# A delta-rule attention with a hardswish feed-forward on one core: one relu of each block a unit later, and the last results in joined stores

## The chip, the cores and the metric

The kernel runs on one core of one Trainium2 chip. The metric is device time in microseconds, from launch to end. A profile of one execution is used beside it; its span runs from the first to the last instruction of the program.

## The reference

```python
for t in range(S):                                   # attention: B=4, H=8, S=768, D=48
    kt, vt, bt = k_n[:, :, t], v[:, :, t], beta[:, :, t, None]     # k_n: keys by their norm
    y[:, :, t] = einsum('bhd,bhde->bhe', q[:, :, t], state)
    v_old = einsum('bhde,bhd->bhe', state, kt)
    state = state + bt[..., None] * einsum('bhd,bhe->bhde', kt, vt - v_old)
x = y.transpose(0, 2, 1, 3).reshape(B * S, H * D)    # 3072 tokens of 384
h = x @ w_in                                         # 384 x 2048
g = h * clip(h + 3, 0, 6) / 6
out = g @ w_out                                      # 2048 x 384, out is 3072 x 384, float32
```

## The kernel before

**Steps and blocks.** The sequence is cut into N = 24 steps `t` of C = 32 tokens. A step holds the 32 tokens of all four batches, 128 rows, which fill the 128 partitions: batch by batch, 32 partitions each. Two steps (CB = 2) make a block of 256 rows, `blk` from 0 to 11, and the feed-forward part runs by blocks. `chain(t)` is the sequential part of a step on TensorE, with copies on ScalarE (ACT) and sums on VectorE (DVE). Its last part, the generator `output()`, makes `y`, transposes it on TensorE into the PSUM tile `yt` (L873), and ScalarE copies that to the step's half of the block's `xT` (L877). In `y` the batches of a pair stand exchanged: batch b is on the partitions of b ^ 1 (`of_heads(py, lambda b: b ^ 1, ...)`, L857).

**The first product.** From block UF = 5 on, `up_by_eleven(blk)` makes x @ w_in. It takes 2 x 2 parts of the operands with seven products in place of eight, and the third 128 rows of w_in with four more: eleven in all. `token_sums(blk)` (L1056, DVE) makes the sums of tokens that this needs out of `xT`, just before. The work is split into NPR = 8 pairs `j` of columns. Of a pair, `begin(j)` issues the first four products into a PSUM bank `ph` (L1066), a copy to `g` on ScalarE (L1080) and two sums on GpSimd (L1030); `end(j)` issues the rest and two sums on DVE (L1093, L1097). Then the pair has two more pieces, which `go(j)` calls one after the other:

- `first`: ScalarE copies the last quarter out of the bank (L1100), which sets the bank free, and makes relu(g / 6 + 1/2) into a scratch tile (L1104).
- `rest`: DVE makes min(relu, 1) times g (L1107, called `go(j)` a second time).

The scratch tile `ro` has the name `o` and one buffer, and so has the tile `o` of the block's results. The first relu of a block therefore waits for the stores of the previous block, and each relu for the L1107 of the pair before it.

**The second product.** From block 2 on `down_by_seven(blk)` makes g @ w_out by seven products (L1218), with copies out of PSUM on ScalarE (L1225) and sums of the parts (L1228) on GpSimd, or on DVE in the last block. Its results stand in `o`, 128 rows by two steps by 384. `to_dram(t, o)` (L1143) stores one step's: a DMA for each batch, 32 rows of 384 floats, all on SP's queue, in the last two steps the odd batches on ScalarE's queue.

**Order.** The order of instructions is written by the program. For the first five steps it is the string `ORDER`; from step LS = 5 on, each step has NU = 15 units: in each, `plan[u]` issues pieces of attention (the chain, and `prep` of a later step: transposes of keys and queries on TensorE into `pt`, L524, and their copies `KQ` on ScalarE, L532), and then `take(units)` issues one unit of the feed-forward part. The yields in `up_by_eleven` part its units. Each engine runs its instructions in the order of issue, and waits for semaphores where an operand is not ready. PSUM banks of the tag `pm` (four) are shared by `ph`, `pt`, `po`, `pz`, `py` and `yt`.

Of the kernel before, what the change touches and what calls it, by code (L numbers as in the profile page):

```python
# [14 lines left out]
ACTF = mybir.ActivationFunctionType  # L15
# [29 lines left out]
def kernel(  # L45
# [21 lines left out]
    nc = tc.nc  # L67
    B, H, S, D = q.shape
    DM, FF = moe_w_in.shape
    C, DP = 32, 64  # L70
    P = B * C
    assert P == 128 and S % C == 0 and D <= DP and H % 2 == 0
    N = S // C
# [6 lines left out]
    CB = 2  # L80
# [14 lines left out]
    def rows(b):  # L95
        return slice(C * b, C * b + C)
# [40 lines left out]
    def needs(*what):  # L137
        assert past.issuperset(what), (what, set(what) - past)
# [5 lines left out]
    def ring(tag, n, key):  # L144

        held = rings.setdefault(tag, [])
        i = len(held)
        if i < n:
            held.append(key)
        else:  # L150
            i = min(range(n), key=lambda i: reads.get(held[i], len(reads)))
            needs(("read", held[i]))
            held[i] = key
        slot[tag] = f"{tag}{i}"

    def read(*keys):
        for key in keys:
            past.add(("read", key))
            reads.setdefault(key, len(reads))
# [53 lines left out]
    for j, value in enumerate((1.0, -1.0)):  # L213
        m = mask2[:, j, :]
        for b in range(B):
            nc.gpsimd.memset(mask2[rows(b), j, :], value)
            nc.gpsimd.affine_select(
                out=mask2[rows(b), j, :], in_=mask2[rows(b), j, :], pattern=[[1, C]],
# [96 lines left out]
    for i, n in enumerate((0, 1, 2, 3, 4, 5, 0, 1, 3, 4, 5, 0, 1, 5, 0, 1)):  # L315
        s, f = weights[i][0].shape[1:]
# [458 lines left out]
    xTs, outs, zs = {}, {}, {}  # L775
# [8 lines left out]
    def by_pair(t):  # L784
        return t.rearrange("p (a e w) -> p e a w", e=2, w=D)

    def chain(t, whole=True):
# [29 lines left out]
        def plus(out, ph, sign, into):  # L817
            for e in range(2):
                nc.vector.scalar_tensor_tensor(
                    out=by_pair(out)[:, e], in0=ph[:, e], scalar=sign, in1=by_pair(into)[:, e],  # L820
                    op0=ALU.mult, op1=ALU.add,
                )

        def of_heads(ps, place, m, z, at=lambda h: h):
            for h in range(H):
                for b in range(B):
                    nc.tensor.matmul(  # L827
                        ps[rows(place(b)), D * h : D * h + D],
                        lhsT=m(h)[rows(b)], rhs=z[rows(b), D * at(h) : D * at(h) + D],
                        start=True, stop=True, skip_group_check=True,  # L830
                        tile_position=(C * b, C * place(b)),
                    )
# [4 lines left out]
        def output(Z=None):  # L837

            if t > 0:
                needs(("turned", t - 1))  # L840
            y = work.tile([P, DM], FP32, name="y", bufs=1)
            if t > 0:
                nc.scalar.activation(
                    out=by_pair(y[:]), in_=even, func=ACTF.Copy, scale=parity[:, 1, 1:2]
                )
                past.add(("even", t))
                if ("R", t) in past:
                    read(("ks", t, 0))
                yield 1
                plus(y[:], odd, parity[:, 0, 1:2], y[:])  # L850
                read(*(("ks", t, i) for i in range(2)))
                yield
            needs(("Z", t))
            Z = zs.pop(t)
            ring("pm", NPM, ("py", t))
            py = psM.tile([P, 512], FP32, name="py", tag=slot["pm"])
            of_heads(py, lambda b: b ^ 1, lambda h: LB[:, he(h), :], Z)  # L857
            past.add(("BZ", t))
            yield
            if t == 0:  # L860
                nc.scalar.activation(out=y[:], in_=py[:, 0:DM], func=ACTF.Copy)
            else:
                nc.vector.tensor_tensor(out=y[:], in0=y[:], in1=py[:, 0:DM], op=ALU.add)
            read(("py", t))
            yield
            blk, cc = divmod(t, CB)
            if cc == 0:
                needs(*([("up", blk - 2)] if blk >= 2 else []))
                xTs[blk] = work.tile([128, NKT, TB], FP32, name="xT")
            ring("pm", NPM, ("yt", t))  # L870
            pt = psM.tile([128, NKT, P], FP32, name="yt", tag=slot["pm"])
            for s in range(NKT):
                nc.tensor.transpose(pt[:, s, :], y[:, s * 128 : (s + 1) * 128], ident[:])  # L873
            past.add(("turned", t))
            yield 1
            read(("yt", t))
            nc.scalar.activation(  # L877
                out=xTs[blk][:, :, cc * P : (cc + 1) * P], in_=pt[:], func=ACTF.Copy
            )
            past.add(("seam", t))  # L880
            yield

# [11 lines left out]
        else:  # L894
# [5 lines left out]
            for e in range(2):  # L900
                nc.vector.scalar_tensor_tensor(
                    out=Rp[:, e].rearrange("p (a w) -> p a w", w=D), in0=even[:, e],
# [4 lines left out]
            if whole:  # L907
                yield
            nc.vector.scalar_tensor_tensor(
                out=Rp, in0=odd.rearrange("p e a w -> p e (a w)"), scalar=parity[:, 1, 0:1],  # L910
# [43 lines left out]
        for i, x in enumerate(su):  # L954
            sv = state[:, 2 * i : 2 * i + 2].rearrange("p b a w -> p b (a w)")
            nc.vector.tensor_tensor(
                out=sv, in0=sv, in1=x[:, :, 0 : NP * D], op=ALU.subtract
# [101 lines left out]
    def up_by_eleven(blk):  # L1059
        needs(("sums", blk))  # L1060
        B11, T3x, B21, B22, _, _ = x_tiles(blk)
        B3 = xTs[blk][:, 2].rearrange("p (i c) -> p i c", c=P)
        phs, ready = {}, {}

        def mm(ph, n, w, x, start=False, stop=False):
            nc.tensor.matmul(  # L1066
                ph[:, n], lhsT=w, rhs=x, start=start, stop=stop, skip_group_check=True
            )

        def begin(j):  # L1070
            key = ("ph", blk, "by", j)
            ring("pm", NPM, key)
            ph = phs[j] = psM.tile([128, 4, P], FP32, name="ph", tag=slot["pm"])
            mm(ph, 0, W11[:, j], B11, start=True)
            mm(ph, 1, S1[:, j], T1x)
            mm(ph, 2, W21[:, j], T3x)
            mm(ph, 3, S2[:, j], T2x)
            gs[blk, j] = g_all[:, 2 * j : 2 * j + 2]
            gt = gs[blk, j].rearrange("p i (t c) -> p (i t) c", c=P)
            nc.scalar.activation(out=gt, in_=ph[:], func=ACTF.Copy)  # L1080
            plus_minus(gt[:, 3:1:-1], gt[:, 0:2], gt[:, 3:1:-1], ALU.add)
            plus_minus(gt[:, 0], gt[:, 0], gt[:, 2], ALU.add)

        def end(j):
            ph = phs.pop(j)
            mm(ph, 0, W12[:, j], B21)
            mm(ph, 1, S4[:, j], B22)
            mm(ph, 2, W22[:, j], T4x)
            mm(ph, slice(0, 2), W13[:, j], B3)
            mm(ph, slice(2, 4), W23[:, j], B3, stop=True)  # L1090
            g = gs[blk, j].rearrange("p i c -> p (i c)")
            gt = gs[blk, j].rearrange("p i (t c) -> p (i t) c", c=P)
            nc.vector.tensor_tensor(  # L1093
                out=gt[:, 1:3], in0=ph[:, 1:3],
                in1=gt[:, 3].unsqueeze(1).to_broadcast([128, 2, P]), op=ALU.add,
            )
            nc.vector.tensor_tensor(out=gt[:, 3], in0=ph[:, 3], in1=gt[:, 0], op=ALU.add)  # L1097

            def first():
                nc.scalar.activation(out=gt[:, 0], in_=ph[:, 0], func=ACTF.Copy)  # L1100
                read(("ph", blk, "by", j))
                ro = mlp.tile([128, CB, DM], FP32, name="o", bufs=1)
                r = ro[:].rearrange("p c m -> p (c m)")[:, 0 : 2 * TB]
                nc.scalar.activation(out=r, in_=g, func=ACTF.Relu, bias=half, scale=1.0 / 6.0)  # L1104

                def rest():
                    nc.vector.scalar_tensor_tensor(  # L1107
                        out=g, in0=r, scalar=1.0, in1=g, op0=ALU.min, op1=ALU.mult
                    )

                ready[j] = rest

            ready[j] = first
            if j == NPR - 1:
                past.add(("up", blk))

        def go(j):
            if j in ready:
                ready.pop(j)()

        begin(0)
        yield
        begin(1)
        yield
        for j in range(NPR):
            end(j)
            go(j - 1)
            if j + 2 < NPR:
                yield
                begin(j + 2)  # L1130
                go(j)
                yield
            else:
                go(j)
                if j == NPR - 1:
                    go(j)
                yield

    def to_dram(t, o):
        for b in range(B):  # L1140
            r0 = b * S + t * C
            eng = nc.scalar if t >= N - CB and b % 2 else nc.sync
            eng.dma_start(out=out[r0 : r0 + C, :], in_=o[rows(b ^ 1)])  # L1143

    def down(blk, c, f0):

# [294 lines left out]
    with tc.manual_schedule():  # L1441
# [15 lines left out]
        for t in range(LS, N):  # L1457
            g, i = group(t)
# [29 lines left out]
            ready = (2, 0) if behind or i == 2 and t - LS == LA - LE else (1, 6)  # L1488
# [62 lines left out]
```

## Time and profile before

| | |
|---|---|
| median of 3 runs | 667.11 us (666.32 to 667.86) |
| profiled execution | 665.93 us, its span 664.1 us |
| mean granted TensorE clock | 0.974 |
| TensorE (PE) | 636.2 us busy, 96% of the span |
| DVE, ACT, POOL | 487.1, 272.1 and 203.5 us busy |
| DMA queues | q1 (SP) 31.29 MB, q10 (ScalarE) 0.30 MB |
| stores to `out` | 92 from SP, 4 from ScalarE, 48.0 KB each |

A line of a timeline has the start in us from the span's start, the duration, the engine, the source line, the operation, output <- inputs and shapes, the count of merged instructions, and in brackets the idle time of the engine just before and what ended it. A line of the waits has who waited, for whom, the us in total, the times and the longest. SPq and ACTq are the instruction queues of SyncE and ScalarE, which issue DMAs; they are not counted as busy. PEld is the load of weights into TensorE.

### The profile page before, as it was taken

Reading aid. Unit: us, or ns where it says so; the run is one execution under the profiler, and the core shown is the slowest. Engines: PE = TensorE matmul, PEld = TensorE weight load, DVE = VectorE, ACT = ScalarE, POOL = GpSimd, SP = SyncE. Lnnn points to the kernel's source line nnn. Section 1 sums busy time; section 2 is a strip of 40 time slices with the busy share of each in tenths; the row PEclk is TensorE's granted clock in tenths of the full one; section 3 lists DMA queues with packets and bytes.
Section 4 is the critical chain, followed back from the end, with each engine's and each line's share of the span. In section 5 each row is a group of like instructions: output and inputs, shape, how many; then the busy total and the mean of one; then the engine's idle time right before and its main releaser. Section 6 shows DMA issues by size and latency. Waiting matters only on the chain.

```text
span 664.1 us, 26330 instructions
## 1 busy us (share of the span) xinstructions
PE 636.2 (96%) x11544; PEld 568.1 (86%) x11544; DVE 487.1 (73%) x1146; ACT 272.1 (41%) x532; POOL 203.5 (31%) x320
## 2 busy tenths in 40 slices
PE   2769999999999999999999999999999999999997
PEld 1658987776789989989989999999999999999997
DVE  4899867898555697657979748989658998456353
ACT  5897679331233143142144244244244144153350
POOL 6531112003511320562254354064052241331430
PEclk9659999999999999999999999999999999999999
DMA  7897246212140030041030030020020020000000
GB/s 175 206 236 197 76 98 161 49 28 41 23 83 8 10 66 3 2 85 27 2 74 3 2 74 3 3 61 2 3 50 2 2 50 1 23 19 2 25 1 25
DMA packets 88499, 33.27 MB, mean 50 GB/s; under 512 B 80160, under 2 KB 83232, under 8 KB 88384
## 3 DMA queue, kind: packets, MB, share of 16 engines
q1 hardware_dynamic: 88128, 31.29, 20.9%
q8 instruction: 91, 1.49, 0.9%
q10 hardware_dynamic: 256, 0.30, 0.2%
q14 instruction: 24, 0.20, 0.1%
HBM read 26.84 MB, written 4.72 MB: 48 GB/s over the span
## 4 chain that ended last, share of the span: by engine, by line
PE 90%; DVE 3%; DMA 2%; SPq 2%; ACT 1%; issue 1%; POOL 0%; ACTq 0%; DVEq 0%; POOLq 0%
PE po L1218 28%; PE ph L1066 20%; PE ph L994 16%; PE po L1154 6%; PE ks L806 3%; PE pt L524 3%; PE su L938 3%; PE pz L827 3%; PE py L827 3%; PE sc L547 3%; PE yt L873 1%; DMA spare<-in_moe_w_in_dram 1%; PE pi L684 1%; DMA w_out<-in_moe_w_in_dram 1%; SPq L168 1%
## 5 line engine op out<-in xcount | busy, mean ns | idle before, releaser
L1066 PE MATMUL ph<-xT,w_in 128*128 128x128 f32 (+1 forms) x560 | 121.4, 321 | 0.7 <-ACT KQ L532 0.5
L994 PE MATMUL ph<-xT,w_in 128*128 128x256 f32 (+1 forms) x576 | 117.1, 353 | 0.9 <-ACT xT L877 0.6
L1218 PE MATMUL po<-w_out,g 128*128 128x192 f32 x640 | 110.6, 326 | 0.0
L994 PEld LDWEIGHTS ph<-xT,w_in 128*128 128x128 f32 x576 | 95.2, 194 | 13.9 <-ACT xT L877 1.0
L1218 PEld LDWEIGHTS po<-w_out,g 128*128 128x128 f32 x640 | 104.6, 190 | 0.5
L1066 PEld LDWEIGHTS ph<-xT,w_in 128*128 128x128 f32 x560 | 91.1, 191 | 5.9 <-ACT KQ L532 0.7
L1030 POOL TENSOR_TENSOR g<-g 128x256 f32<-128x256 f32 x112 | 67.9, 608 | 83.2 <-ACT g L1080 78.8
L1218 PE MATMUL po<-spare,g 128*128 128x192 f32 x480 | 86.7, 332 | 0.0
L1218 PEld LDWEIGHTS po<-spare,g 128*128 128x128 f32 x480 | 77.2, 190 | 1.8
L1001 ACT ACTIVATE g<-ph,halves 128x256 f32<-128x256 f32 (+1 forms) x96 | 41.0, 436 | 74.2 <-PE ph L994 74.2
L1228 POOL TENSOR_TENSOR o<-o,u 128x192 f32<-128x192 f32 x18 | 13.2, 731 | 175.8 <-ACT o L1225 97.2
L1080 ACT ACTIVATE g<-ph 128x512 f32<-128x512 f32 x56 | 33.4, 597 | 81.8 <-PE ph L1066 81.8
L1204 DVE TENSOR_TENSOR g<-g 128x512 f32<-128x512 f32 x80 | 55.5, 715 | 5.6 <-PE po L1218 5.6
L759 DVE TENSOR_TENSOR pr<-A 128x30 f32<-128x30 f32 (+9 forms) x150 | 57.5, 383 | 2.7
L764 DVE TENSOR_TENSOR A<-A,pr 128x30 f32<-128x30 f32 (+9 forms) x150 | 55.7, 371 | 3.7
L1004 DVE SCALAR_TENSOR_TENSOR g<-g,ph 128x256 f32<-128x256 f32 (+1 forms) x96 | 34.7, 371 | 29.4 <-ACT g L1001 29.0
L356 ACT ACTIVATE spare<-spare,places 128x768 uint16<-128x768 uint16 (+1 forms) x56 | 52.6, 944 | 2.8 <-DMA kf<-in_k_dram 1.7
L1093 DVE TENSOR_TENSOR g<-ph,g 128x256 f32<-128x256 f32 x56 | 23.5, 420 | 38.5 <-PE ph L1066 30.9
L1225 ACT ACTIVATE o<-po 128x192 f32<-128x192 f32 x40 | 13.2, 330 | 83.2 <-PE po L1218 79.6
L1154 PE MATMUL po<-w_out,g 128*128 128x384 f32 x128 | 45.2, 491 | 0.0
L1107 DVE SCALAR_TENSOR_TENSOR g<-o,g 128x512 f32<-128x512 f32 x56 | 40.7, 726 | 5.9 <-ACT o L1104 5.9
L1104 ACT ACTIVATE o<-g,halves 128x512 f32<-128x512 f32 x56 | 40.4, 722 | 8.7 <-DVE g L1107 5.7
(141 smaller groups left out, 989.1 us busy)
## 6 DMA issues: line engine op xcount, KB each, us to landing
kf<-in_k_dram SPq DMA_DIRECT2D x96, 48.0 KB, 2.4
qb<-in_q_dram SPq DMA_DIRECT2D x96, 48.0 KB, 2.8
vf<-in_v_dram SPq DMA_DIRECT2D x96, 48.0 KB, 2.2
out_dram<-o SPq DMA_DIRECT2D x92, 48.0 KB, 1.6
spare<-in_moe_w_in_dram SPq DMA_DIRECT2D x4, 768.0 KB, 5.9
w_out<-in_moe_w_in_dram SPq DMA_DIRECT2D x4, 768.0 KB, 6.0
w_out<-in_moe_w_out_dram SPq DMA_DIRECT2D x4, 768.0 KB, 6.9
spare<-in_moe_w_out_dram SPq DMA_DIRECT2D x4, 768.0 KB, 5.0
```

What stands on the lines that cost most here:

```text
L356: nc.scalar.activation(out=z, in_=z if n else d.bitcast(I16)[:, :, :, 3], func=func, bias=places[:, n : n + 1], scale=scale,)
L759: nc.vector.tensor_tensor(out=pv, in0=A[:, j + 1 :, j].unsqueeze(2).to_broadcast([n, w, j]), in1=A[:, j, 0:j].unsqueeze(1).to_broadcast([n ...
L764: nc.vector.tensor_tensor(out=A[:, j + 1 :, 0:j], in0=A[:, j + 1 :, 0:j], in1=pv, op=ALU.subtract)
L994: nc.tensor.matmul(ph[:, cols], lhsT=w_in[:, s, f * 128 : (f + 1) * 128], rhs=xT[:, s, cols], start=(s == 0), stop=(s == NKT - 1),)
L1001: nc.scalar.activation(out=g, in_=ph, func=ACTF.Relu, bias=half, scale=1.0 / 6.0)
L1030: nc.gpsimd.tensor_tensor(out=out, in0=a, in1=b, op=op)
L1066: nc.tensor.matmul(ph[:, n], lhsT=w, rhs=x, start=start, stop=stop, skip_group_check=True)
L1104: nc.scalar.activation(out=r, in_=g, func=ACTF.Relu, bias=half, scale=1.0 / 6.0)
L1107: nc.vector.scalar_tensor_tensor(out=g, in0=r, scalar=1.0, in1=g, op0=ALU.min, op1=ALU.mult)
L1154: nc.tensor.matmul(pos[c][:], lhsT=gs[blk, f // 2][:, f % 2, c * P : (c + 1) * P], rhs=w_out[:, f, :], start=(f == 0), stop=(f == NFC - 1),)
L1204: nc.vector.tensor_tensor(out=A(f, *out, 4), in0=A(f, *a, 4), in1=A(f, *b, 4), op=op)
L1218: nc.tensor.matmul(ps[n][:], lhsT=A(f - f % 2, *a)[:, f % 2], rhs=b[:, f], start=(f == 0), stop=(f == HF - 1),)
```

## The change

Three edits in functions that the order above calls:

- `output()`: in steps 22 and 23 the copy of `yt` into `xT` is made by two instructions, one for each y of a pair of batches, and they put the batches in natural order.
- `up_by_eleven()`: `first` is cut in two. Of pair 0 the copy L1100 stays where it was, and the relu (`second`) is called at the next `go(0)`, one unit later; `rest` of pair 0 is called by a further `go(0)` right ahead of the next `go(1)`. For the other pairs nothing moves.
- `to_dram()`: for steps 22 and 23, two DMAs in place of four. Each takes 64 partitions of `o` and writes two batches of 32 rows: batches 0 and 1 from ScalarE's queue, 2 and 3 from SP's.

```diff
@@ output()
-            nc.scalar.activation(
-                out=xTs[blk][:, :, cc * P : (cc + 1) * P], in_=pt[:], func=ACTF.Copy
-            )
+            xt = xTs[blk][:, :, cc * P : (cc + 1) * P]
+            if t >= N - CB:
+                xt, pt = (x.rearrange("p s (g y c) -> p s g y c", g=2, y=2) for x in (xt, pt[:]))
+                for y in range(2):
+                    nc.scalar.activation(
+                        out=xt[:, :, :, y ^ 1], in_=pt[:, :, :, y], func=ACTF.Copy
+                    )
+            else:
+                nc.scalar.activation(out=xt, in_=pt[:], func=ACTF.Copy)
@@ up_by_eleven()
             def first():
                 nc.scalar.activation(out=gt[:, 0], in_=ph[:, 0], func=ACTF.Copy)
                 read(("ph", blk, "by", j))
+                if j == 0:
+                    ready[j] = second
+                else:
+                    second()
+
+            def second():
                 ro = mlp.tile([128, CB, DM], FP32, name="o", bufs=1)
...
             if j + 2 < NPR:
                 yield
                 begin(j + 2)
+                if j == 1:
+                    go(0)
                 go(j)
                 yield
@@ to_dram()
+        if t >= N - CB:
+            by_batch = out.rearrange("(g y s) m -> g y s m", g=2, y=2)
+            for g, eng in enumerate((nc.scalar, nc.sync)):
+                eng.dma_start(
+                    out=by_batch[g][:, t * C : t * C + C, :], in_=o[2 * C * g : 2 * C * g + 2 * C]
+                )
+            return
         for b in range(B):
             r0 = b * S + t * C
-            eng = nc.scalar if t >= N - CB and b % 2 else nc.sync
-            eng.dma_start(out=out[r0 : r0 + C, :], in_=o[rows(b ^ 1)])
+            nc.sync.dma_start(out=out[r0 : r0 + C, :], in_=o[rows(b ^ 1)])
```

## The prediction

> **What bounds the kernel now.** I read the page first, for the busiest engine and for the chain that ended last.
>
> ```profile
> PE 636.2 (96%) x11544; PEld 568.1 (86%) x11544; DVE 487.1 (73%) x1146; ACT 272.1 (41%) x532; POOL 203.5 (31%) x320
> ...
> PEclk9659999999999999999999999999999999999999
> ...
> PE 90%; DVE 3%; DMA 2%; SPq 2%; ACT 1%; issue 1%; POOL 0%; ACTq 0%; DVEq 0%; POOLq 0%
> ```
>
> TensorE sets the time: it is 96% busy, it is 90% of the chain, and from the fourth slice on its clock is full. A change off TensorE can win only what TensorE waits for, and what follows its last product. So next the waits of TensorE from 290 us on, where all seven blocks with eleven products lie, and the chain of the last 44 us in order of time:
>
> ```profile
> PE ph L1066 <- ACT KQ L532: 0.5, 1, 0.5
> PE ph L1066 <- issue: 0.3, 1, 0.3
> ```
>
> ```profile
> 642.13 18.21 PE po L1218 x112
> 660.35 0.02 issue
> 660.37 0.35 DVE o L1228
> ```
>
> TensorE waits twice in 374 us, for 0.48 us (at 341.10 us) and 0.26 us. The first is all that a reordering of ScalarE can win. The chain's last compute ends at 660.73 us and the span at 664.14 us: 3.4 us of stores and closing. The timeline of the end and the SP queue's waits in it:
>
> ```profile
> 659.67 1.90 SPq L1143 DMA_DIRECT2D out_dram<-o  x4
> 659.68 1.93 ACTq L1143 DMA_DIRECT2D out_dram<-o  x4
> ```
>
> ```profile
> SPq L1546 <- DMA out_dram<-o: 1.5, 1, 1.5
> ```
>
> Eight stores of 48 KB leave, four from each queue: step 23's are issued from 659.67 us, step 22's from 660.76 us. By the trace's packets the first row moves at 660.49 us, the last packet ends at 662.68 us, and what follows takes 1.46 us. The stores' end is therefore the program's end, microsecond for microsecond.
>
> **The change part by part.** The sum is made against the profiled execution: span 664.14 us, 665.93 us with what lies around it. The median of the three runs is 667.11 us, 1.18 us above; I add the difference to the median.
>
> *The two copies of xT in steps 22 and 23.* Each one copy of 384 elements (L877, 490 ns) becomes two of 192. The nearest row is L1225, 192 elements, 330 ns, so two cost 0.66 us, 0.17 us more. The strided read costs nothing extra by L532, which reads a rearranged 512 in 0.60 us like the plain L1080. In step 23 the copy ends at 620.59 us and the token sums on DVE follow it; the third, ending at 622.35 us, feeds the matmuls at 622.94 us. Behind the copy ScalarE has nothing until 623.59 us. Cover 0.59 us against 0.17 us: cost nothing, and 0.17 us if the cover were gone.
>
> *The moved relu.* Its scratch tile shares the buffer of the previous block's results, so the first relu of a block waits for eight stores. The timeline at block 5:
>
> ```profile
> 339.84 0.72 ACT L1104 ACTIVATE o<-g,halves 128x512 f32<-128x512 f32 x1 [0.83 <-ACT g L1100]
> ...
> 340.46 1.06 ACT L532 ACTIVATE KQ<-pt 128x512 f32<-128x512 f32 x2
> ...
> 341.10 0.49 PE L1066 MATMUL ph<-xT,w_in 128*128 128x128 f32 x2 [0.48 <-ACT KQ L532]
> ```
>
> ScalarE sat 0.83 us ahead of L1104. The copy L532 of the transposed keys, ready since 338.64 us, was queued behind that and the relu, and the bank that it frees was what TensorE waited for. A unit later the relu stands behind this L532: the copy then ends near 339.6 us and the 0.48 us go. Next late there is TensorE itself, in the transposes up to 340.61 us. In blocks 10 and 11 the relu also waits (0.54 and 0.40 us), in the other four it does not (0.03 us); TensorE loses nothing in any of the six. Gain: 0.48 us.
>
> The relu's partner on DVE, L1107 (0.68 us), moves too, past the attention step that stands between the units, and the second pair's relu, which overwrites the scratch, is now issued right behind it. Behind a waiting relu on ScalarE stand L1080, L532 and the eviction L1100 of the next pair, and TensorE would wait for these. Relus waited for L1107 16 times in this stretch, 5.7 us in all, 0.6 us at the most, and TensorE for none of that. So I take nothing; the bound is seven blocks by 0.6 us, 4.2 us. DMAs do not move with it.
>
> *The joined stores.* Four transfers of 64 rows replace eight of 32. What matters is how many DMA engines carry one. The page:
>
> ```profile
> q1 hardware_dynamic: 88128, 31.29, 20.9%
> ...
> q10 hardware_dynamic: 256, 0.30, 0.2%
> ```
>
> q10 is ScalarE's queue: four stores of 32 rows and four loads of beta of 8 rows, 160 row packets. The other 96 are of 4 bytes, the writes to semaphores that close a transfer: 4 times 16 and 4 times 8. On q1 the 288 loads of k, q and v, 16 weight loads and 92 stores make 81792 row packets; the remaining 6336 are 396 times 16. So a transfer whose outermost count is 32 or 128 ran on 16 engines, and one whose outermost count is 8 on 8: beta's 3072-byte rows were not cut further. The new store's DRAM side counts batch, row, element, the two batches 768 rows apart: outermost 2. Its SBUF side counts 64 partitions. A share must be cut on both sides, so I take 2 engines, one for each batch, with 32 rows each. The Trainium skill, "DMA: Bandwidth & Descriptors", section "Why a DMA increments its semaphore by 16 and not by 1", states the same as a rule: the engine count is the largest up to 16 that divides both sides' slowest count above 1; beta's 8 agrees, and no transfer of before has unequal counts.
>
> The price of a row follows from the stretch of the last stores:
>
> ```profile
> core 0: us, PE busy (x) PEld busy (x) DVE busy (x) ACT busy (x) POOL busy (x), PEclk, DMA share, GB/s
> 660.40:662.70 2.30, 0.00 (x0) 0.00 (x0) 0.33 (x1) 0.00 (x0) 0.00 (x0) 1.00 0.65 171
> ```
>
> 0.65 of 16 engines over 2.3 us is 23.9 us of engine time for 256 rows and 128 closing writes (9 ns each, 1.2 us): 22.7 us, 89 ns a row; the packets themselves last 62 to 126 ns, mean 87. Whether the two queues use the same two engines no row shows, since both always had all 16. I take the same two, because the queues differ in nothing but the issuer. The same page and section state that this path takes the lowest-numbered engines, which would give the same two; no run here shows it yet.
>
> Then 256 rows lie on 2 engines: 128 rows each, 128 by 87 ns is 11.1 us, from 660.49 us without a pause (the second pair still waits for the same last sum, at 660.73 us, and is issued long before the first is through). End 671.6 us in place of 662.68: 8.9 us. The lower bound is the shortest packet, 62 ns: 7.9 us, so 5.8 us later. The upper one is the pace of weight loads in a stream, 384 rows of 2048 bytes in 3.05 to 3.3 us on 16 engines, 127 to 140 ns; with 133 ns it is 17.0 us, 14.8 us later. I stay at the mean, since it is of these very stores, though two engines alone may move faster than sixteen at once.
>
> Saved issue time (0.4 us a queue) lies ahead of nothing, as the engines are busy by then. Sum: +8.9 - 0.48 = +8.4 us, so 675.5 us.
>
> **The rivals.** *All 16 engines carry each store*, because the 64 partitions decide. For it: 128 and 32 partitions always gave 16. Against it: beta. Then ScalarE's last store is issued at 660.76 in place of 661.17 us; its packets start 1.05 us later as now, four rows an engine take 0.17 us more than two do now (0.32 us), and the end is at 662.3 us, 0.38 us earlier. With the relu that is -0.86 us: 666.2 us, within 0.2%. The Trainium skill speaks for this side in "DMA: Bandwidth & Descriptors", section "Rules for kernel authors": join small transfers into large ones, since under 64 KB mostly overhead is paid; here 48 KB become 96 KB, and beside those 0.38 us no row shows more to win.
>
> *Two engines a store, but others for each queue.* Then an engine has 64 rows, 4.0 to 8.5 us by the same prices, and the stores end 1.8 to 6.3 us later: less 0.48, 668.4 to 672.9 us, at 87 ns 670.0 us. It decides if the second queue counts its engines from another place; that no row shows the engines' numbers leaves it open.
>
> *The relu backfires with the stores harmless.* If the second relu's wait for L1107 pushes L532 or L1080 back by 0.6 us in each of seven blocks: +4.2 - 0.86 + 0.48 = +3.8 us, 670.9 us. Against it: the 16 harmless waits.
>
> **How the numbers follow.** Forecast 0.72: beta is four transfers of four, but with equal sides. Other engines for each queue 0.09, relu 0.03, 16 engines 0.16. A measurement of this kernel tells about 0.2%, 1.3 us, from no change. Of the 0.16 I give 0.13 to no difference and 0.03 to faster, as -0.86 us is under that bound and both of TensorE's waits together would add only 0.26 us. Slower is the rest, 0.84. The range: the forecast's own bounds are 672.4 to 681.5 us (+5.3 to +14.4 us); that is about 0.7 with its tails off, so it reaches down to 668.4 us and takes in the disjoint engines and the relu's case.
>
> **What would show it.** In the profile after: the DMA issues list four stores of 96 KB, landing in 5 us or more in place of 1.6 us; q10 has 196 packets, 2 closing writes to each store (224 would be 16); the mean DMA share is under 0.13 in the last stretch; from the last product to the end some 12.7 us in place of 3.8 us; TensorE has no wait near 341 us. The prediction is wrong if the stores land in about 2 us, or if new waits of TensorE on L532 or L1080 stand in the blocks.

## The result and the profile after

The changed kernel took 674.15 us (median of 6 runs, 672.89 to 675.39), the kernel before 667.43 us beside it: ratio 1.0107, 95% interval 1.0085 to 1.0128. It is slower by 1.07%; the forecast was 675.5 us.

Its profiled execution took 672.89 us, span 671.15 us against 664.14. The page, where it answers to the lines shown of before (busy times, queues, chain):

```profile
PE 633.8 (94%) x11544; PEld 566.6 (84%) x11544; DVE 487.9 (73%) x1146; ACT 272.5 (41%) x534; POOL 205.3 (31%) x320
...
q1 hardware_dynamic: 88068, 31.29, 20.8%
...
q10 hardware_dynamic: 196, 0.30, 0.1%
...
PE 86%; DVE 4%; SPq 4%; DMA 3%; issue 1%; POOL 0%; ACT 0%; DVEq 0%; ACTq 0%; POOLq 0%
```

TensorE works no longer than before (633.8 us against 636.2); it is a smaller share of a longer span. q10 has the forecast 196 packets: two stores of 64 rows, 32 rows of beta, and 36 closing writes, 32 of beta's and 2 for each store. Part of what took the place of TensorE's share is the SP queue (4% of the chain in place of 2%). Its wait for the stores near the end:

```profile
SPq L1566 <- DMA out_dram<-o: 9.1, 2, 6.1
```

Before it waited 1.5 us for the stores, now 9.1 us. The timeline of the end, and the DMA engines' use in a stretch of it (its columns are the stretch, its us, the busy us of five engines, TensorE's clock, the DMA share and GB/s):

```profile
659.33 1.61 SPq L1157 DMA_DIRECT2D out_dram<-o  x2
659.33 1.60 ACTq L1157 DMA_DIRECT2D out_dram<-o  x2
660.03 0.35 DVE L1248 TENSOR_TENSOR o<-u,po 128x192 f32<-128x192 f32 x1 [0.73 <-PE po L1238]
```

```profile
664.00:669.00 5.00, 0.00 (x0) 0.00 (x0) 0.00 (x0) 0.00 (x0) 0.00 (x0) 0.50 0.13 50
```

A share of 0.13 of sixteen engines is two engines, fully busy: 50 GB/s, where the last stores of before had 0.65 and 171 GB/s. By the trace's packets the first row moves at 660.60 us, 1.27 us after its issue, and the last packet ends at 669.92 us. From TensorE's end to the end of the span it takes 11.2 us in place of 3.8; the forecast was 12.7.

TensorE from 290 us on waits once in place of twice, and elsewhere:

```profile
PE yt L873 <- DVE y L863: 0.7, 1, 0.7
```

The first 290 us, in which the start-up loads lie, differ from run to run: TensorE's matmul number 5600, with the same work ahead of it in all, started between 292.1 and 296.9 us in the nine traces of this case, one of each kernel. So I compare from that matmul on. Each cell comes from the trace's times, in us; "closing" is what follows the last packet, up to the end of the span:

| kernel | matmul 5600 to TensorE's end | last sum to last packet | closing | matmul 5600 to the end |
|---|---|---|---|---|
| before | 366.72 | 1.95 | 1.46 | 370.52 |
| after | 366.57 | 9.54 | 1.23 | 377.74 |
| e1, relu alone | 366.42 | 1.97 | 1.43 | 370.21 |
| e2, stores alone | 366.98 | 9.52 | 1.23 | 378.13 |
| e3, rows outermost | 366.41 | 2.11 | 1.24 | 370.15 |
| e4, one store a step | 366.40 | 5.10 | 1.29 | 373.19 |
| e5, one queue | 366.58 | 9.51 | 1.16 | 377.64 |
| e7, relu and hold | 365.76 | 1.97 | 1.55 | 369.67 |
| e8, and halves | 365.79 | 1.68 | 1.31 | 369.17 |

Between TensorE's end and the last sum there are 0.39 us in all of them. So after against before: stores +7.59, TensorE -0.14, closing -0.23, together +7.22 us; the spans differ by 7.02 us, since the start-up was 0.20 us shorter in this execution.

### The profile page after: what moved, and what is told of

Read it like the earlier page. It is cut to its first block, busy times and chain, and to the rows that moved or that the text cites. A ratio compares the mean times of both kernels' runs of the same rounds, so it can differ in the third digit from the quotient of the medians.

```text
span 671.2 us, 26322 instructions
## 1 busy us (share of the span) xinstructions
PE 633.8 (94%) x11544; PEld 566.6 (84%) x11544; DVE 487.9 (73%) x1146; ACT 272.5 (41%) x534; POOL 205.3 (31%) x320
## 4 chain that ended last, share of the span: by engine, by line
PE 86%; DVE 4%; SPq 4%; DMA 3%; issue 1%; POOL 0%; ACT 0%; DVEq 0%; ACTq 0%; POOLq 0%
PE po L1238 28%; PE ph L1072 18%; PE ph L1000 15%; PE po L1174 6%; PE ks L806 3%; PE py L827 3%; PE pz L827 3%; PE pt L524 3%; PE su L944 3%; PE sc L547 2%; DMA spare<-in_moe_w_in_dram 2%; SPq L168 1%; SPq L180 1%; PE yt L873 1%; DMA w_out<-in_moe_w_in_dram 1%
## 5 line engine op out<-in xcount | busy, mean ns | idle before, releaser
L1036 POOL TENSOR_TENSOR g<-g 128x256 f32<-128x256 f32 x112 | 69.6, 623 | 81.3 <-ACT g L1086 76.9
L764 DVE TENSOR_TENSOR A<-A,pr 128x30 f32<-128x30 f32 (+9 forms) x150 | 57.5, 383 | 3.7
L1119 DVE SCALAR_TENSOR_TENSOR g<-o,g 128x512 f32<-128x512 f32 x56 | 40.2, 718 | 6.0 <-ACT o L1116 6.0
```

Of the source, the lines that this page charges most:

```text
L764: nc.vector.tensor_tensor(out=A[:, j + 1 :, 0:j], in0=A[:, j + 1 :, 0:j], in1=pv, op=ALU.subtract)
L1036: nc.gpsimd.tensor_tensor(out=out, in0=a, in1=b, op=op)
```

## The experiments

Theory: the outermost counts of the store's two sides set how many engines carry it; 2 engines make the end, and the relu is a small thing beside it. Rivals: a store of 96 KB to two places is slow by itself; the queue matters; part of the loss is the relu's.

**e1: the moved relu alone.** `output()` and `to_dram()` are those of before.

> The moved relu alone; copies and stores as before. Theory (the relu sets one transfer of keys free earlier, and what it wins is given back where DVE is the limit): TensorE is 0.75 us ahead after block 5's first pairs, loses its lead to one wait of `yt` for DVE's sum `y` in step 20 (0.7 us), and ends 0.2 to 0.5 us earlier than before; the time is within 0.2% of before. Rival (the relu costs): new waits of TensorE on L532 or L1086 in several blocks, some 0.6 us each, 0.5% or more slower. Rival (the give-back is chance): no wait in step 20, TensorE ends about 1 us earlier.

Measured: 666.05 us against 666.88 us, ratio 0.9987 (0.9965 to 1.0008). The interval includes no change, as it would for a gain of a third of a microsecond. TensorE's waits are the single line of after, for `y` in step 20. The traces against each other, matmul by matmul: TensorE gains 0.75 us at block 5 (at 341.1 us of before) and 0.42 us near 397 us, and loses 0.87 us at `yt` of step 20, where before it had none; 0.30 us remain. No wait on L532 or on the begun pairs' copies appears. Both halves of the theory hold in this trace, the lead and the give-back.

**e2: the stores alone.** The copies and `to_dram()` of the change, `first` of before.

```diff
             def first():
                 nc.scalar.activation(out=gt[:, 0], in_=ph[:, 0], func=ACTF.Copy)
                 read(("ph", blk, "by", j))
-                if j == 0:
-                    ready[j] = second
-                else:
-                    second()
-
-            def second():
                 ro = mlp.tile([128, CB, DM], FP32, name="o", bufs=1)
...
                 begin(j + 2)
-                if j == 1:
-                    go(0)
                 go(j)
```

> The joined stores and the copies that they need, the relu as before. Theory: the stores are all of the loss: TensorE ends where it did before (its wait of 0.48 us at 341 us stands), the last packet some 9.3 us after the first row, the span 7.2 to 7.6 us longer than before, ratio 1.010 to 1.012. Rival (part of the loss is the relu's): the span is under 6 us longer.

Measured: 674.36 us, ratio 1.0106 (1.0080 to 1.0131), as the whole change. Its waits of TensorE are before's two, shorter at block 5 and longer at the other:

```profile
PE ph L1072 <- issue: 0.8, 1, 0.8
PE ph L1072 <- ACT KQ L532: 0.2, 1, 0.2
```

The span is 8.4 us longer than before's, over the forecast 7.6; 0.8 us of that is start-up, and from matmul 5600 it is 7.61 us. The stores are the loss, all of it. Up to step 22 this kernel does the same work in the same order as before, so TensorE's two waits also show how much one trace differs from another: 0.19 against 0.48 us at block 5, 0.84 against 0.26 us at the other. A gain of some tenths of a microsecond that is read from one pair of traces is uncertain by as much. From matmul 5600 to TensorE's end, the two kernels without the moved relu take 366.72 and 366.98 us, the five with the moved relu and no hold 366.40 to 366.58.

**e3: the same store with 32 rows outermost.** The copies put the two batches of a pair in turn, row by row, so one store still takes 64 partitions and two batches.

```diff
-                xt, pt = (x.rearrange("p s (g y c) -> p s g y c", g=2, y=2) for x in (xt, pt[:]))
+                xt = xt.rearrange("p s (g c y) -> p s g y c", g=2, y=2)
+                pt = pt[:].rearrange("p s (g y c) -> p s g y c", g=2, y=2)
...
-            by_batch = out.rearrange("(g y s) m -> g y s m", g=2, y=2)
+            by_batch = out.rearrange("(g y s) m -> g s y m", g=2, y=2)
...
-                    out=by_batch[g][:, t * C : t * C + C, :], in_=o[2 * C * g : 2 * C * g + 2 * C]
+                    out=by_batch[g][t * C : t * C + C], in_=o[2 * C * g : 2 * C * g + 2 * C]
```

> As the change, but the copies of xT put the two batches of a store row by row in turn, so that the store's DRAM side counts 32 rows outermost, then the 2 batches; SBUF side, bytes, rows, count of stores and queues are the change's. Theory (the outermost counts of both sides set the number of engines): 16 engines, 64 packets of rows and 16 closing writes to each store, the last packet 1.5 to 2 us after the first row, TensorE's lead of some 0.3 us kept, together 0.3 to 0.9 us faster than before, ratio 0.9985 to 1.000. Rival (a store of 96 KB, or one to two separate places, is slow by itself): as the change, 674 us. Rival (always few engines for a three-count pattern): the same 674 us.

Measured: 666.45 us against 666.88 us, ratio 0.9995 (0.9975 to 1.0014). The whole loss is gone with bytes, rows, stores and queues unchanged. Its queues, and the engines' use in the last stretch:

```profile
q1 hardware_dynamic: 88096, 31.29, 21.2%
...
q10 hardware_dynamic: 224, 0.30, 0.1%
```

```profile
659.00:661.10 2.10, 0.00 (x0) 0.00 (x0) 0.00 (x0) 0.00 (x0) 0.00 (x0) 0.90 0.67 187
```

224 packets on q10 are 16 closing writes a store, as forecast for 16 engines, and 0.67 of the engines work in place of 0.13. That a store of 96 KB is slow by itself falls. But joining wins nothing either: from the last sum to the last packet it is 2.11 us against 1.95. A joined store's issue takes 0.54 to 0.66 us in place of 0.31 to 0.46, and from SP's queue its first row moves 1.2 to 1.3 us after the issue in place of 0.8 to 1.0.

**e4: one store a step for all four batches**, from SP.

```diff
-            by_batch = out.rearrange("(g y s) m -> g y s m", g=2, y=2)
-            for g, eng in enumerate((nc.scalar, nc.sync)):
-                eng.dma_start(
-                    out=by_batch[g][:, t * C : t * C + C, :], in_=o[2 * C * g : 2 * C * g + 2 * C]
-                )
+            by_batch = out.rearrange("(b s) m -> b s m", b=B)
+            nc.sync.dma_start(out=by_batch[:, t * C : t * C + C, :], in_=o)
```

> As the change, but one store a step, 128 partitions to four batches, both from SP's queue: the DRAM side counts 4 outermost. Theory (outermost counts): 4 engines, 4 closing writes to each of the two stores, 64 rows an engine at 61 ns, 3.9 us, with a slow start of up to 1.5 us: the last packet 4 to 5.5 us after the first row, 670 us, ratio 1.003 to 1.006. Rival (two engines a queue, whatever the counts): 128 rows an engine, as the change or slower, 674 us. Rival (the 128 partitions of the SBUF side decide): 16 engines, 666.5 us.

Measured: 670.20 us, ratio 1.0050 (1.0031 to 1.0070). The stretch of its last rows:

```profile
664.00:666.50 2.50, 0.00 (x0) 0.00 (x0) 0.00 (x0) 0.00 (x0) 0.00 (x0) 0.50 0.27 100
```

0.27 of sixteen are four engines, with twice the GB/s of two. First row to last packet: 4.87 us, in the forecast 4 to 5.5. The 128 partitions of the SBUF side did not bring sixteen, so the SBUF side alone does not decide; and one queue with four engines beats two queues with two.

**e5: the change with both pairs of stores from SP's queue** (`enumerate((nc.sync, nc.sync))`).

> As the change, but all four joined stores from SP's queue. Theory (two engines of the same numbers carry the stores of either queue, and their rows of 61 ns set the end): as the change, last packet 8.5 to 10.5 us after the first row, span some 7 us longer than before. Rival (the queues share the load, or the switching between them costs): the end moves by over 1.5 us against the change.

Measured: 676.27 us in its one run, whose start-up was the longest of all (matmul 5600 at 296.9 us). From there to the end it took 377.64 us, the change 377.74; first row to last packet 9.30 us against 9.33. The queue does not matter in this one trace, which fits two engines that are the same for both queues.

**e7: the moved relu, and DVE's queue cut at the place of the give-back.** To e1 it adds that in step 20 no inverse step follows unit 8:

```diff
-                if i == 1 == ready[0] and 5 < u < 7:
+                if (i == 1 == ready[0] and 5 < u < 7) or (t, u) == (20, 8):
                     continue
```

> The moved relu, stores and copies as before, and in step 20 the two inverse steps (L759, L764 with 150 elements) that DVE made right ahead of the sum y stand behind it. Theory (what the relu wins is given back where DVE's queue is the limit): TensorE's wait for y in step 20 is gone, its lead against before after the start-up stays near 1.1 us in place of 0.3 us, ratio 0.997 to 0.999. Rival (DVE's work is only pushed on): another wait for DVE of 0.5 us or more appears in step 20 or 21, and the end is as with the moved relu alone.

Measured: 667.12 us against 667.96 us beside it, ratio 0.9991 (0.9972 to 1.0010): the time alone tells nothing. The traces do. DVE's timeline before, in the change, and in e7, each with the transposes of step 20 that need the sum `y`:

```profile
548.63 0.32 DVE L764 TENSOR_TENSOR A<-A,pr 128x150 f32<-128x150 f32 x1
548.87 0.55 DVE L863 TENSOR_TENSOR y<-y,py 128x384 f32<-128x384 f32 x1
...
549.83 0.49 PE L873 MATMUL yt<-ident,y 128*128 128x128 f32 x3
```

```profile
548.12 0.73 DVE L764 TENSOR_TENSOR A<-A,pr 128x150 f32<-128x150 f32 x1
548.77 0.54 DVE L863 TENSOR_TENSOR y<-y,py 128x384 f32<-128x384 f32 x1
...
549.46 0.52 PE L873 MATMUL yt<-ident,y 128*128 128x128 f32 x3 [0.71 <-DVE y L863]
```

```profile
549.48 0.33 DVE L764 TENSOR_TENSOR A<-A,pr 128x168 f32<-128x168 f32 x1
549.73 0.55 DVE L863 TENSOR_TENSOR y<-y,py 128x384 f32<-128x384 f32 x1
...
550.67 0.49 PE L873 MATMUL yt<-ident,y 128*128 128x128 f32 x3
...
552.72 0.32 DVE L764 TENSOR_TENSOR A<-A,pr 128x150 f32<-128x150 f32 x1
```

In the change y starts when the step of 150 elements is done; in e7 that step comes 3 us later. TensorE's only wait there is now

```profile
PE pz L827 <- DVE R L909: 0.2, 1, 0.2
```

one step later, so 0.24 us of the 0.87 us are still given back, and 0.96 us remain of what the relu won (365.76 us against 366.72). The forecast 1.1 us was a little high; TensorE waits for DVE in step 21 too.

**e8: e7, and step 22's results stored in two halves of columns.** The first 192 columns leave by four stores from SP while the last products run, the other 192 at the end.

```diff
+        if blk + 1 == N // CB:
+            to_dram(blk * CB, o[:, 0], slice(0, HM), False)
         copy(C12, 7)
...
-        to_dram(blk * CB, o[:, 0])
+        to_dram(blk * CB, o[:, 0], slice(HM if blk + 1 == N // CB else 0, DM))
```

> As e7, and step 22's results are stored in two halves of columns: the first, ready early, by four stores from SP during the last products, the second (rows of 768 bytes) at the end as before from both queues. Theory (the last stores are bound by their issue and first row, not by bytes): the last packet 0.1 to 0.3 us earlier after the last sum than the 1.95 us of before; ratio 0.996 to 0.999. Rival (bytes count): 0.5 us or more earlier.

Measured: 666.66 us against 667.96 us, ratio 0.9981 (0.9961 to 1.0001); from matmul 5600 it takes 1.35 us less than before. TensorE has 0.93 us of this, the stores 0.27, the closing 0.15. The last packet comes 1.68 us after the last sum in place of 1.95: half the bytes of the stores that wait for the last sum are worth 0.27 us. By this all their bytes would be worth 0.54 us, an estimate, so most of that end is not theirs. By the two ratios it beats the changed kernel by 1.2%; that it beats the one before is what its trace shows, while its interval just includes no change.

## Why the prediction was right

**How many engines.** Right, and what decided it: 2 engines for counts of 64 and 2. e4 and e3 carry the step further, 4 for 128 and 4, and 16 for 64 and 32. The Trainium skill, "DMA: Bandwidth & Descriptors", section "Why a DMA increments its semaphore by 16 and not by 1", gives all three by the largest number up to 16 that divides both sides' slowest counts; the traces of stores with unequal sides agree with it, by 2, 4 and 16 closing writes. They do not show that both sides count: in every one of these stores the DRAM side has the smaller count, so a rule on the DRAM side alone would give 2, 4 and 16 as well. No store with the smaller count on the SBUF side was run, and none with a count that would tell "the largest divisor" from "the smaller count".

**Whether the queues share them.** Right: 0.13 of sixteen with both queues at work, and e5. The same section's lowest-numbered engines would give that; no trace of this case numbers the engines.

**The price of a row.** This is the term that was mis-sized. The forecast took 87 ns, the mean of packets of sixteen engines at once, and 11.1 us for 128 rows. Two engines alone move a row each 61 ns (most packets last 65 ns), close to the 62 ns of the lower bound: 7.8 us. On top come 1.5 us that the forecast did not have: ten rows, all of them in the first 2.7 us, take 0.22 to 0.46 us each, which is 1.2 us an engine more than at 65 ns; the rest are small gaps. Together 9.3 us, between the lower bound and the value taken, 1.8 us under it. The first row moved 1.27 us after its issue in place of 0.82, 0.45 us that the forecast did not have either. So from the last sum the last packet came 7.59 us later in place of 8.9 (7.24 us on the clocks of the two spans, with start-up and TensorE's lead in it). What makes those first rows slow was not tried. Two readings behind the prices were off: the last 256 rows of before last 90 ns in the mean, not 87, and the loads of 384 weight rows took 3.05 to 5.07 us from first packet to last, not up to 3.3 (and 3.3 us for 24 rows an engine are 138 ns, not 140). The first would have made the forecast 0.35 us higher and so further off, the second the upper bound higher.

**The second pair.** Right: issued at 660.41 us, it waited for engines, not they for it.

**The sum.** It came out nearer than its terms. Forecast were +8.4 us, the traces give +7.2 from matmul 5600 on: the stores were 1.3 us too dear, the relu 0.3 us too hopeful, and a closing 0.2 us shorter was not in the sum. The errors of the stores and of the relu partly cancel, and that is luck.

**The relu.** The place and the way were right: the copy L532 now stands ahead of the relu,

```profile
338.69 0.60 ACT L532 ACTIVATE KQ<-pt 128x512 f32<-128x512 f32 x1
...
339.58 0.72 ACT L1116 ACTIVATE o<-g,halves 128x512 f32<-128x512 f32 x1 [0.28 <-ACT KQ L532]
```

and TensorE's wait at block 5 is gone, worth 0.75 us where 0.48 was forecast, since the start of the matmul behind the wait gains 0.65 us and the next one 0.10. The 0.48 us are one trace's: in e2, with the relu where it was, the wait was 0.19 us. What failed is the sentence that TensorE itself is next late. DVE was: in step 20 it works without a pause, its sum `y` came at the same time with and without the relu's lead (549.3 and 549.4 us, with start-ups 0.2 us apart), and 0.87 us of the lead went there. The forecast looked at what TensorE waited for, not at the slack of DVE where it did not: 0.41 us between the end of y and the transposes before. e7 shows that this is the cause.

**The second wait** of before, 0.26 us on "issue" near 397 us, was left alone in the forecast. It is listed for no kernel with the moved relu, and it grew to 0.84 us in e2. In before and e2, which wait, the matmul behind it starts 1.4 and 1.5 us after a packet of 16 KB on the instruction queue ended, so it may be a wait for instructions. But in the change, e1 and e3, which do not wait, the same distance is 1.4, 1.5 and 1.3 us. What it is stays open.

**The copies and L1107.** Nothing on TensorE waits for the two copies of step 23 or for the later L1119 (the L1107 of before), as taken. The two copies last 0.33 us each and 0.55 us together, as they overlap, against 0.66 forecast. Relus wait for L1119 23 times in place of 16, 8.2 us in place of 5.7, and TensorE for none of that: the harmless side of the forecast's bound.

**The rivals.** That all engines carry a store, at -0.86 us, was wrong in its premise, and e3, which makes the premise true, shows that its price was off as well: -0.37 us from matmul 5600, of which 0.31 are TensorE's and 0.22 a shorter closing, while the stores' end came 0.16 us later. The rows' price was right there (86 ns in the mean), but the joined store's longer issue and later first row were not in the sum. The relu's backfire did not come; what came was smaller and in another engine.

## What to carry to other kernels

Before two stores are joined, write down the outermost count of both sides: the pattern that began with "2 batches" ran on two DMA engines, though 32 rows of each followed, and at the end of this program nothing hid that. The same rows with 32 outermost ran on sixteen and cost nothing against before, and the count of closing 4-byte packets in the profile tells which it was. Here a lead won for the busiest engine lasted to the next place where another engine had less slack than the lead, so read that slack before the gain is counted.

## What the runs showed of the hardware that was not expected

- Two DMA engines moved 50 GB/s between them, four 100 GB/s, 25 GB/s each in rows of 1536 bytes; sixteen in the short last burst 171 to 187 GB/s, 11 to 12 GB/s each over the stretch.
- ScalarE's store, issued 5 ns after SP's, had its first row moved 4.2 us after its issue (663.52 us), when 50 of SP's 64 rows on the same engines had begun. From then on, while both had rows, the two queues took turns, row by row.
- Early rows of a store on two or four engines were slow, up to 0.48 us each in place of 0.065 us; on two engines they cost 1.2 us an engine.
- The time to reach the same matmul after the start-up loads differed by 4.8 us between the nine traces, more than the relu, the hold and the halves together are worth (1.35 us). What makes it was not tried.
